# A second Strassen level over pairs of inner blocks in the gate and up products

## The chip, the cores and the metric

One core of a Trainium2 chip runs one program. The metric is the device time of an execution in microseconds (us); several executions are timed, and the median is compared. One further execution was recorded by the hardware profiler: its trace gives the start and the length of each instruction on each engine (TensorE or PE, VectorE or DVE, ScalarE or ACT, GpSimd or POOL, SyncE or SP) and of each DMA.

## The reference, cut to what matters

```python
g = sigmoid((x * gate_w).sum(-1, keepdims=True))       # x: 2048 x 640
a = Cr @ (x @ Wr.T) - Ci @ (x @ Wi.T)                  # C: 2048 x 2048, W: 640 x 640
b = (gelu(x @ w_gate) * (x @ w_up)) @ w_down           # inner width 1728
return g * a + (1 - g) * b
```

All in float32. The change lies in the products with w_gate and w_up.

## The kernel before

The kernel works transposed: the 640 features lie in five blocks of 128 partitions, the 2048 tokens in four tiles of T = 512 columns. Two neighbouring tiles make a token pair (tp 0 and 1). Every float32 operand is split in two parts, a high one (`high`, a copy on ACT to the type fp32r) and the rest (`low`, a subtraction on DVE), and each product is three matmuls (`mm3`, lines 85 to 87): high by high, high by low, low by high, each 128x128 by 128x512 into one PSUM bank.

The inner width 1728 is 13 blocks of 128 and a rest. Block 0 and the rest are done plainly at the start. For each of the blocks f = 1 to 12, `gate_up` (line 271) computes the gate's and the up part's output for one token pair by one level of Strassen's scheme in Winograd's form: the left matrix is the two by two of (gate, up) by (features 0 and 1, features 2 and 3), the right one is (the same features) by (the two token tiles); feature 4 is added plainly (`u5`, `g5`, `D`). Seven products of two feature blocks go to the banks X, Z and V. The sums of the left side come from `load_w` (line 198), the sums T1 to T4 of the right side were made at the start by `load_x`. gate_up is a generator of seven steps, and the loop takes a step of token pair 0 and one of token pair 1 in turn:

A11 to X (copied to s1); S1 and u5 to Z (copied to s5); S2 added to X (copied to s2); A12 and g5 to V (s1 += V, gelu); S3 added to X (s5 += X); S4 and D added to Z (s2 += Z, gelu, times s5); A22 and u5 added to X (s1 *= X).

Two blocks, 2k + 1 and 2k + 2, are one unit for the next product: their outputs and some differences of them go through `keep` (a DMA on POOL's queue) to the DRAM tensors hA and hT, from which the next stage, the product with w_down (`load_k`, `split_k`, `step_k`), loads them. The differences of the second block need s2 and s5 of the first, which are held in `hid`.

Around these products the loop does other stages' work: `sum_wd` and `sum_wu` load weights of later products, form four sums and write them to DRAM; `load_z` loads a block of 128 tokens, multiplies it by the gate row (line 390) and adds it up (line 391); `gate_rows` makes the gate from that. Before the change there is one such sum and up to two gate tiles behind each block.

All larger tiles share one ring of 48 slots of 4 KB a partition (`slot`, `pair`), tiles of 512 columns share 12 (`mtile`), small weight tiles 4 (`wsmall`), and all PSUM tiles the 8 banks (`bank`). An instruction that writes a new tile, or a DMA that fills one, waits until a slot of the ring has no more readers. In the loop the order of each engine's instructions is made by the program's planner from the order of the code and its own durations; SP issues the loads in one order and waits for each one's slot.

Of the kernel before, what the change touches and what calls it, by code (L numbers as in the profile page):

```python
# [29 lines left out]
def kernel(  # L30
# [82 lines left out]
    h0 = [dram.tile([P, 4, T], F32, tag=f"h0{p}", name=f"h0{p}") for p in range(2)]  # L113
    wsu, wneg = ([dram.tile([P, 8, P], F32, tag=f"{n}{p}", name=f"{n}{p}") for p in range(ND)] for n in ("wsu", "wneg"))
    uA, uT = ([[dram.tile([P, 4, T], F32, tag=f"u{n}{j}{p}", name=f"u{n}{j}{p}") for p in range(ND)] for j in range(2)] for n in "AT")
    grd, gmd = (dram.tile([1, S], F32, tag=n, name=n) for n in ("grd", "gmd"))
# [82 lines left out]
    def load_w(f):  # L199
        ra, *a = wchunk(f"wa{f}")  # L200
        rb, d = wsmall(F32, f"wb{f}"), wsmall(F32R, f"wd{f}")
        nc.sync.dma_start(ra, wf[f - 1, :, :8])
        nc.sync.dma_start(rb, wf[f - 1, :, 8:])
        sm, *c = wchunk(f"ws{f}")
        g01, g23, u23 = ra[:, 0:2], ra[:, 2:4], ra[:, 5:7]
        high(a[0], ra)
        tt(sm[:, 0:2], rb, u23, op=ALU.add)
        tt(sm[:, 4:6], g01, rb, op=ALU.subtract)
        tt(sm[:, 2:4], sm[:, 0:2], g01, op=ALU.subtract)
        tt(sm[:, 6:8], g23, sm[:, 2:4], op=ALU.subtract)  # L210
# [12 lines left out]
        return W  # L223

    def keep(to, i, src):
        nc.gpsimd.dma_start(to[:, i], src)  # L226
# [51 lines left out]
    def gate_up(f, W, B, tp, s5):  # L278
# [53 lines left out]
            hid[tp] = s2, s5  # L332
        yield

    def sums_left(n, r, a21, to):

        sm = slot(F32, [P, 8, P], f"{n}s")
        a11, a12, a22 = r[:, 0:2], r[:, 2:4], r[:, 6:8]
        tt(sm[:, 0:2], a21, a22, op=ALU.add)
        tt(sm[:, 4:6], a11, a21, op=ALU.subtract)  # L340
        tt(sm[:, 2:4], sm[:, 0:2], a11, op=ALU.subtract)
        tt(sm[:, 6:8], a12, sm[:, 2:4], op=ALU.subtract)
        nc.gpsimd.dma_start(to, sm)

    def sum_wd(k):

        r, a21 = slot(F32, [P, 8, P], f"dr{k}"), wsmall(F32, f"da{k}")
        nc.sync.dma_start(r, wd[k, :, :8])
        nc.sync.dma_start(a21, wd[k, :, 8:])
        sums_left(f"d{k}", r, a21, wsd[k])  # L350

    def sum_wu(p):


        r, a21 = slot(F32, [P, 8, P], f"ur{p}"), wsmall(F32, f"ua{p}")
        nc.sync.dma_start(r, wu[p, :, :8])
        nc.sync.dma_start(a21, wu[p, :, 8:])
        if p > 1:
            v, r = r, slot(F32, [P, 8, P], f"un{p}")
# [95 lines left out]
    def load_k(i):  # L455


        tp, b, k = kseq[i]
        n = f"{tp}{b}{k}"
        if k == NK and b:  # L460
            return
        r = slot(F32, [P, 8, P], f"kw{n}")
        if k == NK:
            m = slot(F32, [P, 8, P], f"km{n}")
            nc.sync.dma_start(r[:, :5], wd0)
            for q in range(2):
                nc.sync.dma_start(m[q * FR : (q + 1) * FR, :5], wdr)
            r, src = (r, m), h0[tp]
        elif b:
            nc.sync.dma_start(r[:, 0:2], wd[k, :, 6:8])  # L470
            nc.sync.dma_start(r[:, 2:8], wsd[k][:, 0:6])
            src = hT[tp][k]
        else:
            nc.sync.dma_start(r[:, 0:6], wd[k, :, 0:6])
            nc.sync.dma_start(r[:, 6:8], wsd[k][:, 6:8])
            src = hA[tp][k]
        raw = []
        for q in range(2):
            raw.append(pair(F32, f"kr{n}{q}"))
            nc.sync.dma_start(raw[q], src[:, 2 * q : 2 * q + 2])  # L480
        kraw[i] = r, raw

    def split_k(i):
        tp, b, k = kseq[i]
        n = f"{tp}{b}{k}"
        if k == NK and b:
            ktile[i] = ktile[("left", tp)]
            return
        r, raw = kraw.pop(i)
        W = {}  # L490
# [207 lines left out]
        plain_gate_up(W0, B, 1, 2)  # L698
    Bs.append(B)
    zq = list(range(NS))  # L700
    for f in range(1, NF):
        nxt = load_w(f + 1) if f + 1 < NF else None
        s5 = pair(F32, f"s5{f}")
        work = [gate_up(f, W, Bs[tp], tp, s5[:, tp]) for tp in range(2)]
        for step in range(7):
            for w in work:
                next(w)
            if f == NF - 1:
                if step == 1:
                    split_k(0)  # L710
                if step >= 4:
                    load_k(step - 3)
        if f % 2:
            sum_wd(f // 2)
        elif f <= 2 * ND:
            sum_wu(f // 2 - 1)
        if f == NF - 2:
            gate_rows()
            gm = [gate_tile(gmd, tp, f"gm{tp}") for tp in range(2)]
            load_k(0)  # L720
        for _ in range(2):
            if f > 1 and zq:
                load_z(zq.pop(0))
        W = nxt
    order = ctx.enter_context(ExitStack())
    order.enter_context(in_order(ACT, DVE))
    split_k(1)
# [354 lines left out]
```

## Time and profile before

| | us |
|---|---|
| median of 3 runs | 1030.92 |
| lowest and highest run | 1030.63, 1032.3 |
| the profiled execution | 1031.27 |
| its span, from the first instruction to the last | 1029.5 |

The rows below come from the page of the profiled execution and from answers of its trace. A group of instructions is given by line, engine, operation and tiles; its busy time and the mean length of one stand behind the bar, and then the idle time of the engine just before it. Matmuls overlap, so the distance between two starts tells more than the length of one.

### The profile page before, as it was taken

How to read it: one execution, taken by the hardware profiler on the slowest of the kernel's cores; microseconds unless marked ns; L12 is line 12 of the kernel's file. 1: busy time of each engine (PE TensorE's matmuls, PEld its weight loads, DVE VectorE, ACT ScalarE, POOL GpSimd, SP SyncE). 2: the span in 40 equal slices, each digit the busy share in tenths (PEclk: the TensorE clock that was granted, in tenths of full speed). 3: DMA queues.
4: the chain of work that ended last, by engine and by line, in shares of the span. 5: the costliest groups of instructions: out<-in, count | busy, mean ns of one | idle time of the engine just before them, and what ended most of it. 6: DMA issues, size and time to landing. Idle time of an engine off the chain costs nothing.

```text
span 1029.5 us, 12790 instructions
## 1 busy us (share of the span) xinstructions
PE 1023.9 (99%) x4530; PEld 846.2 (82%) x4530; DVE 770.6 (75%) x1030; ACT 449.6 (44%) x570; POOL 132.2 (13%) x237
## 2 busy tenths in 40 slices
PE   9999999999999999999999999999999999999998
PEld 7888888888888888888888888888888888888887
DVE  6998675767654967986798975796678769697775
ACT  5453334343523546556345443343344344365430
POOL 0012121212121200100010011002000200021013
PEclk9999999999999999999999999999999999999999
DMA  8246644746446997878866577557656878897748
GB/s 299 74 153 219 221 169 160 239 160 240 154 148 215 381 346 242 276 253 287 288 216 206 209 224 280 178 198 245 257 177 217 273 275 278 288 328 212 283 94 133
DMA packets 78609, 234.05 MB, mean 227 GB/s; under 512 B 10096, under 2 KB 18320, under 8 KB 78544
## 3 DMA queue, kind: packets, MB, share of 16 engines
q1 hardware_dynamic: 57968, 169.31, 48.6%
q0 software_dynamic: 20432, 63.73, 18.4%
q8 instruction: 35, 0.57, 0.2%
q14 instruction: 30, 0.25, 0.1%
q10 hardware_dynamic: 144, 0.20, 0.1%
HBM read 169.21 MB, written 63.98 MB: 227 GB/s over the span
## 4 chain that ended last, share of the span: by engine, by line
PE 98%; DMA 1%; DVE 0%; ACT 0%; issue 0%; SPq 0%; ACTq 0%
PE pX L85 8%; PE pX L86 8%; PE pX L87 8%; PE pZ L86 5%; PE pZ L85 5%; PE pZ L87 5%; PE pV L86 3%; PE pV L85 3%; PE pV L87 3%; PE pL L85 3%; PE pL L87 3%; PE pL L86 3%; PE pY L87 1%; PE pY L85 1%; PE pR L87 1%; PE pR L85 1%
## 5 line engine op out<-in xcount | busy, mean ns | idle before, releaser
L74 ACT ACTIVATE ch<-csa 128x1024 fp32r<-128x1024 f32 x32 | 34.0, 1063 | 88.4 <-DVE csa L436 53.4
L131 ACT ACTIVATE s<-pX 128x512 f32<-128x512 f32 x64 | 37.8, 596 | 77.2 <-PE pX L87 69.2
L74 ACT ACTIVATE ch<-cra 128x1024 fp32r<-128x1024 f32 x32 | 33.9, 1058 | 47.4 <-PE pL L86 21.6
L77 DVE TENSOR_TENSOR cl<-crb,ch 128x1024 fp32r<-128x1024 f32 x32 | 39.1, 1221 | 17.0 <-ACT ch L74 9.7
L77 DVE TENSOR_TENSOR cl<-cra,ch 128x1024 fp32r<-128x1024 f32 x32 | 39.1, 1222 | 15.5 <-ACT ch L74 15.1
L86 PE MATMUL pL<-cl,xah 128*128 128x512 f32 x128 | 49.8, 389 | 0.0
L87 PE MATMUL pL<-ch,xal 128*128 128x512 f32 x128 | 49.8, 389 | 0.0
L85 PE MATMUL pL<-ch,xah 128*128 128x512 f32 x128 | 49.3, 389 | 0.0
L226 POOL DMA_DIRECT2D hA<-s x48 | 26.1, 544 | 177.0 <-DVE s L313 170.6
L303 DVE TENSOR_TENSOR s<-s,pV 128x512 f32<-128x512 f32 x24 | 16.3, 683 | 41.8 <-PE pV L87 17.6
L77 DVE TENSOR_TENSOR cl<-csb,ch 128x1024 fp32r<-128x1024 f32 x32 | 39.2, 1224 | 6.3 <-ACT ch L74 4.7
L74 ACT ACTIVATE ch<-crb 128x1024 fp32r<-128x1024 f32 x32 | 33.8, 1055 | 21.0 <-DVE cl L77 7.8
L77 DVE TENSOR_TENSOR cl<-csa,ch 128x1024 fp32r<-128x1024 f32 x32 | 39.1, 1221 | 4.0 <-ACT ch L74 3.3
L74 ACT ACTIVATE ch<-csb 128x1024 fp32r<-128x1024 f32 x32 | 33.9, 1059 | 11.9 <-PE pL L86 6.9
L77 DVE TENSOR_TENSOR kl<-kw,kh 128x1024 fp32r<-128x1024 f32 (+1 forms) x26 | 31.4, 1208 | 10.0 <-ACT kh L74 10.0
L74 ACT ACTIVATE kh<-kw 128x1024 fp32r<-128x1024 f32 (+1 forms) x26 | 27.3, 1048 | 11.6 <-DMA kw<-wsd 7.3
L312 ACT ACTIVATE s<-s 128x512 f32<-128x512 f32 x24 | 15.2, 633 | 38.8 <-DVE s L311 38.8
L788 POOL DMA_DIRECT2D uA<-s x16 | 8.7, 542 | 159.3 <-DVE s L834 152.5
L87 PEld LDWEIGHTS pL<-ch,xal 128*128 128x128 f32 x128 | 24.0, 188 | 5.0
L86 PEld LDWEIGHTS pL<-cl,xah 128*128 128x128 f32 x128 | 24.0, 188 | 5.0
L85 PEld LDWEIGHTS pL<-ch,xah 128*128 128x128 f32 x128 | 24.0, 188 | 5.0
L226 POOL DMA_DIRECT2D hT<-s x48 | 26.0, 543 | 14.9 <-DVE s L317 3.9
(3584 smaller groups left out, 3332.6 us busy)
## 6 DMA issues: line engine op xcount, KB each, us to landing
cra<-in_ct SPq DMA_DIRECT2D x64, 512.0 KB, 3.9
crb<-in_ct SPq DMA_DIRECT2D x64, 512.0 KB, 4.8
hA<-s POOLq DMA_DIRECT2D x48, 256.0 KB, 4.7
hT<-s POOLq DMA_DIRECT2D x48, 256.0 KB, 4.8
kr<-hA SPq DMA_DIRECT2D x24, 512.0 KB, 7.8
kr<-hT SPq DMA_DIRECT2D x24, 512.0 KB, 6.5
ux<-uA SPq DMA_DIRECT2D x24, 512.0 KB, 5.5
ux<-uT SPq DMA_DIRECT2D x16, 512.0 KB, 7.1
```

Of the source, the lines that this page charges most:

```text
L74: nc.scalar.activation(hi, raw, AF.Copy)
L77: nc.vector.tensor_tensor(lo, raw, hi.bitcast(F32), op=ALU.subtract)
L85: nc.tensor.matmul(ps, lh, rh, start=first, stop=False, skip_group_check=True)
L86: nc.tensor.matmul(ps, lh, rl, start=False, stop=False, skip_group_check=True)
L87: nc.tensor.matmul(ps, ll, rh, start=False, stop=last, skip_group_check=True)
L131: nc.scalar.activation(m, src, AF.Copy)
L226: nc.gpsimd.dma_start(to[:, i], src)
L303: tt(s1, s1, V, op=ALU.add)
L312: nc.scalar.activation(s2, s2, AF.Gelu_apprx_tanh)
L788: nc.gpsimd.dma_start(to[:, i], src)
```

## The change

Blocks 3 to 12 are taken in five pairs. `gate_up` stays for blocks 1 and 2. In a pair, the first products of both blocks with both token pairs (A11 and A12 of gate_up) are one two by two matrix of features by blocks times one of features by token pairs, and `pair_first` does them by seven products for each of the features' two halves J, where there were eight. A product's running sum is copied on by ACT from one PSUM bank to a new one (`seed`), into which matmuls go on adding. `chain` and `last_products` do what is left of gate_up for one block and one token pair in four steps: S1, S2, S3, and S4 with A22.

The left side's sums over the two blocks are made by `pair_parts`; `chain_parts` and `plain_parts` make what `load_w` made. The right side's sums over the two token pairs are made once by `cross_sums`, during blocks 1 and 2: one stays in place of a part of x that is no longer needed, three for each J are written to DRAM (`xtd`), and each pair loads the six again by `load_cross`, into slots of the ring.

The other stages' sums and gate tiles are moved into the first block of each pair (`extras`, eleven of them), gate_rows and the first load of the next stage into the middle and the end of block 11. A gate tile's product and its addition are one instruction. wsmall has six tiles, and `warm` takes a slot of the ring.

```diff
@@ wsmall, load_z, warm
-        return pool.tile([P, 2, P], dt, tag="w", name=name, bufs=4)
+        return pool.tile([P, 2, P], dt, tag="w", name=name, bufs=6)
...
-        nc.vector.tensor_tensor(r, r, gwb, op=ALU.mult)
-        nc.vector.tensor_reduce(z[:, sb : sb + 1], r, axis=mybir.AxisListType.X, op=ALU.add)
+        nc.vector.tensor_tensor_reduce(r, r, gwb, 1.0, 0.0, ALU.mult, ALU.add, z[:, sb : sb + 1])
...
-    warm = pool.tile([P, T], BF16, tag="warm", name="warm")
+    warm = slot(BF16, [P, T], "warm")
@@ weights of a pair
+    def chain_parts(f, raw, W):
...
+        sm, *c = wchunk(f"ws{f}")
...
+        split(*c, sm)
+        tt(rb[:, 1], ra[:, 4], ra[:, 7], op=ALU.subtract)
+        split(d[:, 0], d[:, 1], rb[:, 1])
...
+    def plain_parts(f, ra):
+        a = slot(F32R, [P, 2, 4, P], f"wp{f}")
+        split(a[:, 0], a[:, 1], ra[:, 4:8])
...
+    def pair_parts(p, r0, r1):
+        a, b = (r[:, 0:4].rearrange("q (j k) c -> q k j c", j=2) for r in (r0, r1))
+        sm = slot(F32, [P, 4, 2, P], f"vs{p}")
+        h, l = slot(F32R, [P, 4, 2, P], f"vh{p}"), slot(F32R, [P, 4, 2, P], f"vl{p}")
+        e, q = slot(F32R, [P, 2, 4, P], f"ve{p}"), pool.tile([P, 2, 2, P], F32R, tag="m", name=f"vq{p}", bufs=12)
...
+        split(h, l, sm)
+        split(e[:, 0], e[:, 1], r0[:, 0:4])
+        split(q[:, 0], q[:, 1], b[:, 1])
@@ sums over the token pairs
+    def cross_sums(J):
+        r = [pair(F32, f"xc{J}{q}") for q in range(2)]
+        for q in range(2):
+            nc.sync.dma_start(r[q], xt[2 * q, 2 * J - 2 : 2 * J].rearrange("d p c -> p d c"))
...
+        for k, (a, b) in enumerate(((h, h2), (l, l2))):
+            nc.gpsimd.dma_start(xtd[J][:, 0:2, k], a.bitcast(F32))
+            nc.gpsimd.dma_start(xtd[J][:, 2, k], b.bitcast(F32))
+        return b12
+    def load_cross(J, i):
+        tcross[J, i] = slot(F32R, [P, 2, T], f"xx{J}{i}")
+        nc.sync.dma_start(tcross[J, i].bitcast(F32), xtd[J][:, {1: 0, 4: 1, 2: 2}[i]])
@@ the products
+    def seed(ps, name):
+        b = bank(name)
+        nc.scalar.activation(b, ps, AF.Copy)
+        return b
+    def pair_first(p, WP, W):
...
+        m(va, 2, "a11", "b11", True)
+        v00 = seed(va, f"pv00{p}")
+        m(xa_, 1, "a11", "b11", True)
+        X[0, 0] = seed(xa_, f"px00{p}")
+        m(ve, 2, "s1", "t1", True)
+        sv = copy(ve, f"sv{p}")
+        m(v00, 2, "a12", "b21")
+        m(xe, 1, "s1", "t1", True)
+        sx = copy(xe, f"sx{p}")
+        m(va, 2, "s2", "t2")
+        v01 = seed(va, f"pv01{p}")
+        m(X[0, 0], 1, "a12", "b21")
+        s1[0, 0] = copy(X[0, 0], f"s100{p}")
+        m(xa_, 1, "s2", "t2")
+        X[0, 1] = seed(xa_, f"px01{p}")
+        fifth(v00, 0, 0)
+        gated(s1[0, 0], v00)
+        m(v01, 2, "s4", "b22")
+        m(va, 2, "s3", "t3")
+        v10 = seed(va, f"pv10{p}")
+        m(X[0, 1], 1, "s4", "b22")
+        tt(X[0, 1], X[0, 1], sx, op=ALU.add)
+        s1[0, 1] = copy(X[0, 1], f"s101{p}")
+        m(xa_, 1, "s3", "t3")
+        X[1, 0] = seed(xa_, f"px10{p}")
+        tt(xa_, xa_, sx, op=ALU.add)
+        X[1, 1] = xa_
+        s1[1, 1] = copy(xa_, f"s111{p}")
+        fifth(v01, 0, 1)
+        gated(s1[0, 1], v01, sv)
+        m(v10, 2, "a22", "t4")
+        fifth(v10, 1, 0)
+        m(X[1, 0], 1, "a22", "t4")
+        s1[1, 0] = copy(X[1, 0], f"s110{p}")
+        gated(s1[1, 0], v10)
+        fifth(va, 1, 1)
+        gated(s1[1, 1], va, sv)
+    def chain(f, W, B, tp, s5, X, s1):
...
+        prod(Z, "S1", "T1", True)
+        mm3(Z, W["u5"], x2, False, True)
+        nc.scalar.activation(s5, Z, AF.Copy)
+        yield
+        prod(X, "S2", "T2", False)
+        s2 = copy(X, f"s2{n}")
+        yield
+        prod(X, "S3", "T3", False)
+        tt(s5, s5, X, op=ALU.add)
+        yield
+        prod(Z, "S4", (2, 2), False)
+        mm3(Z, W["D"], x2, False, True)
+        tt(s2, s2, Z, op=ALU.add)
+        last_products(X, W, B, tp, k, second, s1, s2, s5, prod)
+        yield
@@ the loop over pairs
+    for p in range(1, NK):
+        f = 2 * p + 1
+        for J in (2, 1):
+            load_cross(J, 4)
+        X, s1 = pair_first(p, WP, Ws)
+        for i in range(2):
+            s5 = pair(F32, f"s5{f + i}")
+            work = [chain(f + i, Ws[i], Bs[tp], tp, s5[:, tp], X[i, tp], s1[i, tp]) for tp in range(2)]
+            for step in range(4):
+                for w in work:
+                    next(w)
+                if (i, step) == (0, 0):
+                    chain_parts(f + 1, raws[1], Ws[1])
+                if i == 0 and step in (1, 3):
+                    extras()
...
+                if (i, step) == (0, 2):
+                    nraws = load_raw(f + 2), load_raw(f + 3)
+                if (i, step) == (1, 0):
+                    raws = nraws
+                    WP = pair_parts(p + 1, raws[0][0], raws[1][0])
+                if (i, step) == (1, 1):
+                    nWs = [plain_parts(f + 2 + i, raws[i][0]) for i in range(2)]
+                    for J in (2, 1):
+                        load_cross(J, 1)
+                if (i, step) == (1, 2):
+                    chain_parts(f + 2, raws[0], nWs[0])
+                    load_cross(2, 2)
+                if (i, step) == (1, 3):
+                    load_cross(1, 2)
+                    Ws = nWs
```

## Rows read from the trace of the kernel before

**Rows 1.** The page's parts 1 and 4: busy time of the engines, and the chain.

```profile
PE 1023.9 (99%) x4530; PEld 846.2 (82%) x4530; DVE 770.6 (75%) x1030; ACT 449.6 (44%) x570; POOL 132.2 (13%) x237
...
PE 98%; DMA 1%; DVE 0%; ACT 0%; issue 0%; SPq 0%; ACTq 0%
```

**Rows 2.** All waits of PE: for whom, us in total, times, longest.

```profile
PE pwarm L656 <- DVE warm L613: 1.2, 1, 1.2
PE pm L263 <- ACT x011h L74: 0.5, 1, 0.5
PE kX L85 <- ACT ks L131: 0.3, 1, 0.3
```

**Rows 3.** The table of stretches: block 2, blocks 3 and 4, two of the next stage.

```profile
core 0: us, PE busy (x) PEld busy (x) DVE busy (x) ACT busy (x) POOL busy (x), PEclk, DMA share, GB/s
72.40:96.90 24.50, 24.50 (x110) 20.30 (x109) 20.51 (x38) 9.60 (x15) 4.25 (x9) 1.00 0.61 202
96.20:145.20 49.00, 49.00 (x218) 40.59 (x217) 34.62 (x61) 16.84 (x26) 9.86 (x19) 1.00 0.54 189
...
340.00:360.00 20.00, 20.00 (x90) 16.55 (x89) 18.98 (x20) 12.88 (x14) 4.44 (x9) 1.00 1.04 377
341.10:1029.50 688.40, 684.52 (x3047) 567.51 (x3046) 532.74 (x642) 310.65 (x356) 69.73 (x118) 1.00 0.73 245
```

**Rows 4.** The timeline of PE in block 2 and at its border with block 3.

```profile
85.32 0.39 PE L85 MATMUL pX<-xT03h,ws2h 128*128 128x512 f32 x1
...
88.04 0.39 PE L85 MATMUL pZ<-x022h,ws2h 128*128 128x512 f32 x1
...
95.97 0.39 PE L87 MATMUL pX<-x15h,wa2l 128*128 128x512 f32 x1
96.20 0.39 PE L85 MATMUL pX<-x011h,wa3h 128*128 128x512 f32 x1
```

**Rows 5.** The timeline of PE and of ACT: the end of a product and its copy.

```profile
100.73 0.39 PE L87 MATMUL pZ<-x05h,wa3l 128*128 128x512 f32 x1
...
101.16 0.60 ACT L296 ACTIVATE s<-pZ 128x512 f32<-128x512 f32 x1 [1.44 <-PE pZ L87]
```

**Rows 6.** Groups of DVE by line and shape in blocks 3 and 4.

```profile
L324 DVE TENSOR_TENSOR s<-s,pX 128x512 f32<-128x512 f32 x5 | 3.4, 682 | 0.1
L390 DVE TENSOR_TENSOR xz<-xz,gwb 128x640 f32<-128x640 f32 x4 | 3.3, 816 | 0.0
L391 DVE TENSOR_REDUCE z<-xz 128x1 f32<-128x640 f32 x4 | 3.2, 810 | 0.0
...
L77 DVE TENSOR_TENSOR wa5l<-wa5r,wa5h 128x1024 fp32r<-128x1024 f32 x1 | 1.2, 1218 | 0.0
...
L209 DVE TENSOR_TENSOR ws5r<-ws5r,wa5r 128x256 f32<-128x256 f32 x1 | 0.4, 418 | 0.0
```

**Rows 7.** Groups of ACT by line and shape in blocks 3 and 4.

```profile
L131 ACT ACTIVATE s<-pX 128x512 f32<-128x512 f32 x8 | 4.8, 598 | 10.1 <-PE pX L87 7.3 <-DMA hA<-s 2.8
L312 ACT ACTIVATE s<-s 128x512 f32<-128x512 f32 x4 | 2.5, 634 | 5.5 <-DVE s L311 5.5
...
L74 ACT ACTIVATE ws5h<-ws5r 128x1024 fp32r<-128x1024 f32 x1 | 1.1, 1064 | 0.0
...
L74 ACT ACTIVATE wd<-wb 128x128 fp32r<-128x128 f32 x2 | 0.6, 312 | 5.3 <-DVE wb L213 5.3
```

**Rows 8.** Line 202, the loads of a block's weights (512 KB each): issue to landing.

```profile
DMA to landing us min/median/max: 3.7/5.2/7.3
```

**Rows 9.** The timeline of SP, and SP's waits in the loop for line 202.

```profile
104.46 0.33 SPq L202 DMA_DIRECT2D wa5r<-in_wf  x1
...
SPq L202 <- DMA hT<-s: 15.3, 4, 7.4
```

**Rows 10.** The timeline of PE at the start of the program.

```profile
5.42 0.63 PE L263 MATMUL pg<-x011h,w0h 128*128 128x512 f32 x1
5.84 0.63 PE L263 MATMUL pu<-x011h,w0h 128*128 128x512 f32 x1
```

More of the change, by code (lines that the diff above doesn't have):

```diff
@@ L115 @@
     uA, uT = ([[dram.tile([P, 4, T], F32, tag=f"u{n}{j}{p}", name=f"u{n}{j}{p}") for p in range(ND)] for j in range(2)] for n in "AT")
+    xtd = {J: dram.tile([P, 3, 2, T], F32, tag=f"xtd{J}", name=f"xtd{J}") for J in (1, 2)}
     grd, gmd = (dram.tile([1, S], F32, tag=n, name=n) for n in ("grd", "gmd"))
@@ L223, in load_w, with load_raw @@
         return W
+    def load_raw(f):
+        ra, rb = slot(F32, [P, 8, P], f"wa{f}"), wsmall(F32, f"wb{f}")
+        nc.sync.dma_start(ra, wf[f - 1, :, :8])
+        nc.sync.dma_start(rb, wf[f - 1, :, 8:])
+        return ra, rb
+    def chain_parts(f, raw, W):
+        ra, rb = raw
+        sm, *c = wchunk(f"ws{f}")
+        g01, g23, u23 = ra[:, 0:2], ra[:, 2:4], ra[:, 5:7]
+        tt(sm[:, 0:2], rb, u23, op=ALU.add)
+        tt(sm[:, 4:6], g01, rb, op=ALU.subtract)
+        tt(sm[:, 2:4], sm[:, 0:2], g01, op=ALU.subtract)
+        tt(sm[:, 6:8], g23, sm[:, 2:4], op=ALU.subtract)
+        d = wsmall(F32R, f"wd{f}")
+        split(*c, sm)
+        tt(rb[:, 1], ra[:, 4], ra[:, 7], op=ALU.subtract)
+        split(d[:, 0], d[:, 1], rb[:, 1])
+        W["D"] = d[:, 0], d[:, 1]
+        for i in range(2):
+            for k in range(4):
+                W[f"S{k + 1}", i] = at(c, 2 * k + i)
@@ new lines, in cross_sums @@
+    def cross_sums(J):
+        r = [pair(F32, f"xc{J}{q}") for q in range(2)]
+        for q in range(2):
+            nc.sync.dma_start(r[q], xt[2 * q, 2 * J - 2 : 2 * J].rearrange("d p c -> p d c"))
+        b11, b21, b12, b22 = r[0][:, 0], r[0][:, 1], r[1][:, 0], r[1][:, 1]
+        tt(b11, b12, b11, op=ALU.subtract)
+        tt(b12, b22, b12, op=ALU.subtract)
+        tt(b22, b22, b11, op=ALU.subtract)
+        tt(b21, b21, b22, op=ALU.subtract)
+        h, l = hl(f"xU{J}")
+        split(h, l, r[0])
+        h2, l2 = mtile(F32R, f"xh{J}"), mtile(F32R, f"xl{J}")
+        split(h2, l2, b22)
+        for k, (a, b) in enumerate(((h, h2), (l, l2))):
+            nc.gpsimd.dma_start(xtd[J][:, 0:2, k], a.bitcast(F32))
+            nc.gpsimd.dma_start(xtd[J][:, 2, k], b.bitcast(F32))
+        return b12
@@ L225, in keep @@
+    tcross = {}
+    def load_cross(J, i):
+        tcross[J, i] = slot(F32R, [P, 2, T], f"xx{J}{i}")
+        nc.sync.dma_start(tcross[J, i].bitcast(F32), xtd[J][:, {1: 0, 4: 1, 2: 2}[i]])
     def keep(to, i, src):
@@ L333, in gate_up, with m, fifth, gated @@
         yield
+    def seed(ps, name):
[3 more added lines that the diff above has]
+    def pair_first(p, WP, W):
+        b = {J: {"b11": at(Bs[0][J, 1], 0), "b21": at(Bs[0][J, 1], 1), "b22": at(Bs[1][J, 1], 1), "t3": at(Bs[1][J, 1], 0)} for J in (1, 2)}
+        for J in (1, 2):
+            for i in (1, 2, 4):
+                c = tcross.pop((J, i))
+                b[J][f"t{i}"] = c[:, 0], c[:, 1]
+        def m(ps, J, w, x, first=False):
+            mm3(ps, WP[J][w], b[J][x], first, True)
+        def fifth(ps, f, q):
+            mm3(ps, W[f]["g5"], at(Bs[q][5], 0), False, True)
+        def gated(s1, *more):
+            for v in more:
+                tt(s1, s1, v, op=ALU.add)
+            nc.scalar.activation(s1, s1, AF.Gelu_apprx_tanh)
+        va, xa_, ve, xe = (bank(f"p{n}{p}") for n in ("va", "xa", "ve", "xe"))
+        X, s1 = {}, {}
+        m(va, 2, "a11", "b11", True)
[35 more added lines that the diff above has]
+        gated(s1[1, 1], va, sv)
+        return X, s1
@@ new lines, in chain, with prod @@
+    def chain(f, W, B, tp, s5, X, s1):
+        n = f"{f}_{tp}"
+        Z = bank(f"pZ{n}")
+        x1, x2 = at(B[5], 0), at(B[5], 1)
+        k, second = divmod(f - 1, 2)
+        def prod(ps, a, b, first):
+            for i in range(2):
+                mm3(ps, W[a, i], at(B[b], i), first and i == 0, True)
+        prod(Z, "S1", "T1", True)
[13 more added lines that the diff above has]
+        yield
@@ new lines, in last_products @@
+    def last_products(X, W, B, tp, k, second, s1, s2, s5, prod):
+        nc.scalar.activation(s2, s2, AF.Gelu_apprx_tanh)
+        tt(s2, s2, s5, op=ALU.mult)
+        keep(hA[tp][k], 1 + 2 * second, s2)
+        if second:
+            h12, t1 = hid.pop(tp)
+            tt(h12, s2, h12, op=ALU.subtract)
+            keep(hT[tp][k], 2, h12)
+            tt(t1, s2, t1, op=ALU.subtract)
+            keep(hT[tp][k], 1, t1)
+        prod(X, "A22", "T4", False)
+        mm3(X, W["u5"], at(B[5], 0), False, True)
+        tt(s1, s1, X, op=ALU.mult)
+        keep(hA[tp][k], 2 * second, s1)
+        if second:
+            tt(s5, s1, t1, op=ALU.subtract)
+            keep(hT[tp][k], 3, s5)
+        else:
+            tt(s5, s2, s1, op=ALU.subtract)
+            keep(hT[tp][k], 0, s5)
+            hid[tp] = s2, s5
@@ L700, with extras @@
     zq = list(range(NS))
-    for f in range(1, NF):
-        nxt = load_w(f + 1) if f + 1 < NF else None
+    sq = [lambda k=k: sum_wd(k) for k in range(NK)]
+    for p in range(ND):
+        sq.insert(2 * p + 1, lambda p=p: sum_wu(p))
+    def extras():
+        sq.pop(0)()
+        for _ in range(2):
+            if zq:
+                load_z(zq.pop(0))
+    t3 = {}
+    W2 = load_w(2)
+    for f in (1, 2):
         s5 = pair(F32, f"s5{f}")
@@ L707 @@
                 next(w)
[L708 to L723, printed above, removed]
@@ L724 @@
-        W = nxt
+            if (f, step) in ((1, 3), (2, 0)):
+                J = 3 - f
+                t3[J] = cross_sums(J)
+            if f == 2 and step == 2:
+                raws = load_raw(3), load_raw(4)
+        W = W2
+    WP = pair_parts(1, raws[0][0], raws[1][0])
+    for J in (1, 2):
+        split(Bs[1][J, 1][0][:, 0], Bs[1][J, 1][1][:, 0], t3[J])
+    Ws = [plain_parts(3 + i, raws[i][0]) for i in range(2)]
+    for i in (1, 2):
+        for J in (2, 1):
+            load_cross(J, i)
@@ new lines @@
+    chain_parts(3, raws[0], Ws[0])
+    for p in range(1, NK):
[3 more added lines that the diff above has]
+        X, s1 = pair_first(p, WP, Ws)
+        for i in range(2):
+            s5 = pair(F32, f"s5{f + i}")
[7 more added lines that the diff above has]
+                    extras()
+                if p == NK - 1:
+                    if (i, step) == (0, 2):
+                        extras()
+                        gate_rows()
+                        gm = [gate_tile(gmd, tp, f"gm{tp}") for tp in range(2)]
+                    if (i, step) == (0, 3):
+                        load_k(0)
+                    if (i, step) == (1, 0):
+                        split_k(0)
+                    if i == 1 and step >= 1:
+                        load_k(step)
+                    continue
+                if (i, step) == (0, 2):
+                    nraws = load_raw(f + 2), load_raw(f + 3)
+                if (i, step) == (1, 0):
+                    raws = nraws
+                    WP = pair_parts(p + 1, raws[0][0], raws[1][0])
+                if (i, step) == (1, 1):
+                    nWs = [plain_parts(f + 2 + i, raws[i][0]) for i in range(2)]
+                    for J in (2, 1):
+                        load_cross(J, 1)
[5 more added lines that the diff above has]
+                    Ws = nWs
```

13 lines of the change are left out of this document (added).

## The prediction

> **What bounds the kernel now.** Read the busy times first: TensorE (PE) is busy 99% of the span, VectorE (DVE) 75%, ScalarE (ACT) 44%, and the chain that ended last is 98% PE [rows 1]. A busy PE need not be a PE at its pace, so read the waits next: over the whole span PE waited for others 2.0 us in three places, none of them in the gate/up loop [rows 2]. Then the timeline: matmuls start 0.2267 us apart (12 in 2.72 us), and the last of one block is followed by the first of the next at the same distance [rows 4]. So in this loop each matmul costs 0.2267 us and nothing else costs anything; a change can gain by taking matmuls out, and everything else in it can only lose. Last, the table of stretches: a pair of inner blocks (49.0 us) has DVE at 34.6 us, ACT at 16.8 to 18.3 and the DMA engines at 0.54 of their time with 189 GB/s; the stage behind it also runs PE without a gap [rows 3], so what is gained here stays gained to the end.
>
> **Part 1, matmuls.** Before, one block and one token pair take 18 products of 3 matmuls, 54; two blocks and two token pairs 216. After, pair_first has 14 products `m` and 4 `fifth`, 54 matmuls, and each of four chains 13 products, 39: 54 + 156 = 210. Five pairs (blocks 3 to 12; blocks 1 and 2 keep the old form) save 30 matmuls, 30 x 0.2267 = **6.8 us**. This has one answer.
>
> **Part 2, ACT and DVE work, hidden by their idle time.** Per pair ACT goes from 20 operations of 128x512 to 28 (6 seeds, 6 copies, 4 + 4 gelus, 4 + 4 copies of the chains): 8 x 0.6 = +4.8 us; its splits of weights go from four wide and two narrow ones to three wide, three of 512, one of 256 and two narrow ones, about +1.1 us. That makes ACT some 24 of 47.6 us. DVE goes from 28 additions and products to 32 (+4 x 0.68 = 2.7 us); the weights' sums and low halves from 9.4 to 12.3 us (+2.9); four gate reductions lose one of their two operations, 4 x 0.81 = -3.2 us if the merged one takes what the product takes, 0 if it takes both [rows 6, 7]. So 37 to 40 of 47.6 us. Both stay under PE's time: cost 0. A seed is ACT writing PSUM, which no row shows; the nearest is the PSUM-to-SBUF copy of 0.598 us [rows 7], and I bound it at 0.4 to 1.06 us (the row of the wide split) and take 0.6. In the stretch of block 2 DVE had 20.5 of 24.5 us busy [rows 3]; there the two cross_sums (4.2 us each), the pair's first sums and splits take the place of load_w(3), load_w(4), two sums and two gate tiles, about 17 us for about 17 us: cost 0, and if that cover fails it delays the first pair once, by 1 to 3 us.
>
> **Part 3, new short distances between PE and ACT.** ACT starts 0.43 us after the start of the last matmul of a product (100.73 to 101.16) [rows 5] and takes 0.6, so a copy is done 1.03 us after that start. In pair_first the fourth product needs the first seed; between lie two products, so it starts 7 x 0.2267 = 1.59 us after the same point: 0.56 us of room. The later seeds have 1.2 us or more. In chain, S3 now follows S2 directly (A12 stood between): the copy of X after S2 of one token pair must be done before S3 of that pair, again with 0.56 us of room. That is 5 tight points in a pair, 25 in all. If ACT has just begun a wide split (1.06 us), the point loses 0.5 us: bounds 0 and 12.5 us. Queued behind such a wait is all of PE. ACT has some three wide operations in 47.6 us, so a collision is rare: I take 0.02 us a point, 0.5 us. Nothing suggests a gain here: no wait of PE is left to remove.
>
> **Part 4, the cross tiles, the real risk.** A pair reads six tiles of 512 KB back from DRAM: 3.1 MB on top of 189 GB/s x 49 us = 9.3 MB, so about 260 GB/s, below the 377 that a stretch behind shows with PE full [rows 3]. Bandwidth is no bound; the moment of issue is. A load is issued when one of the 48 slots is free. Count them in step 2 of the second block: 32 hold the split x parts and sums, 1 the gate row; the current pair still holds 2 + 1 weight tiles and two s5; the next pair holds two raw tiles, 3 of pair_parts, 2 of plain_parts and the two first cross tiles: 47. Still wanted before the border are chain_parts' three and two cross tiles. So some wait for the next release: S4's weights of the second block, free 12 matmuls = 2.7 us before the border. Tile (2,2) is first read after 5 products (3.4 us), tile (1,2) after 7 (4.8), (2,4) after 14 (9.5), (1,4) after 16 (10.9). The last two can have the slots that the first two tiles leave at 2.0 and 3.4 us. Room from release to use: 6.1, 7.5, 7.5 and 7.5 us. Loads of 512 KB in this loop landed in 3.7 to 7.3 us, median 5.2 [rows 8], and issuing takes 0.33 [rows 9]. So the median fits everywhere, and the longest is late by 1.5 us at the first. I take 0.25 us a border, 1.0 us for four; the bounds are 0 and the case of rival 1. The Trainium skill, "DMA: Bandwidth & Descriptors", section on the anatomy of one DMA, gives about 2.0 us plus bytes over 436 GB/s; for 512 KB that is an estimate of 3.2 us, every tile would be there, and the sum would be the whole 6.8 us less 0.5. The rows disagree (5.2), and I go by them.
>
> **Part 5, moves.** The down and hidden-DFT sums (loads on SP, writes on POOL) and the gate tiles come as eleven `extras`, two a pair and one more, instead of one a block: the same instructions, past the same queues, in the half of a pair in which no cross tile is needed soon. gate_rows and the first load_k come in the middle of block 11 instead of behind it, so the next stage's loads start earlier: 0. Cross_sums' eight writes are on POOL, which is busy 9.9 of 49 us [rows 3], 20 us and more before they are read. The six small tiles and `warm` in a slot: 0.
>
> **Sum.** 1029.5 us of span - 6.8 + 0.5 + 1.0 = 1024.2. The profiled execution lasted 1031.27, 1.77 more than its span: 1026.0. The median of the runs, 1030.92, lies 0.35 below that execution, so the forecast is **1025.6**.
>
> **Rival 1, slower: cross tiles wait for a slot that a write must empty.** The place is the border of pairs. The other slots in question there are the two s5 tiles, which are written to DRAM at the end of a pair. The trace shows what a load that takes such a slot gets: wa5r was issued at 104.46, though the pair had ended at 96.20 [rows 4, 9], 8.3 us later, and four loads of this line waited for these writes, 15.3 us together [rows 9]. If tile (2,4) gets this slot it lands at 8.3 + 0.3 + 5.2 = 13.8 us, needed at 9.5: 4.3 us, at four borders 17 us, so 1025.6 - 1.0 + 17 = 1042. It decides from 1.4 us lost a pair (6.8 / 5). For it: 52 tiles want 48 slots, and SP issues in order. Against it: six slots come free between -2.7 and +4.2 us (S4's two, the second block's plain tile, three cross tiles) before s5's do, and in the trace such waits never reached PE [rows 2]. Chance 0.17.
>
> **Rival 2, no change: the tight points of part 3 take the gain.** If half the bound is met at each of 25 points (0.25 us), 6.25 us go: about 1030.9 with the rest as summed. For it: ACT has half its time full. Against: what runs there is short, and an operation of 0.6 us in the way costs 0.1 at most. Chance 0.08.
>
> **Rival 3, no change: it does what it says, and the next stage waits out the gain.** PE reaches the down product 6.8 us earlier, in a stretch where the DMA engines are full (1.04, 377 GB/s) and DVE has 19.0 of 20 us busy [rows 3]. If those and not PE set the pace there, the gain is given back: 1030.9. Against: load_k moves forward by more than that, and PE has no wait there now [rows 2]. Chance 0.08.
>
> **Rival 4, slower: the clock.** The trace shows the lower pace once, in the first 7 us, after PE had stood still for data: starts 0.42 us apart, as at 1.2 GHz (the stretch's granted clock doesn't show it), where 0.2267 belongs to 2.4 [rows 10, 4]. Eleven or so matmuls ran so, 0.2 us lost each. If each of five borders brought one such fall, 5 x 2.2 = 11 us: 1036. That needs PE to stand still at the borders, so it comes only behind rival 1 or 2. Chance 0.03. The Trainium skill, "TensorE: Matmul & The Clock Gate", section on psum-queue depth-cycling, has a rule of this kind: cycling through banks makes PE idle briefly between groups, and the clock swings. Before, PE cycles through 12 banks a pair and the granted clock is 1.00 in all stretches [rows 3], so the trace doesn't bear it out.
>
> **How the numbers follow.** The forecast with its losses of 0 to 4 us has 0.64. About 0.2% (2 us) is what a measurement of this kernel can tell from no change. Faster 0.64, same 0.16 (rivals 2 and 3), slower 0.20 (rivals 1 and 4). Low end: the whole 6.8 us from the fastest run, 1023.4 with a little over; high end 1033.0, where rival 1 has lost 2.5 us a border more than forecast; beyond it stay about 0.15 above and 0.04 below.
>
> **What would show it.** Right: 4500 matmuls, PE still at 99%, starts still 0.2267 us apart through pair_first, a pair in 47.6 us instead of 49.0, and PE's waits in the loop under 2 us. Part 3 wrong: waits of PE on ACT at the S3 products or the fourth product of a pair. Part 4 wrong, rival 1: waits of PE for tiles xx, or products of a chain drawn ahead, with SP's loads of xx waiting for the hT writes. Rival 3: the same loop shorter, and waits at the kX, kL products. Rival 4: starts 0.43 us apart behind a border. The count of part 1 is certain; the prediction would be wrong by what PE waits.

## The result and the profile after

The changed kernel took 1034.29 us (median of 9; 1032.22 to 1037.43), the kernel before 1030.92: a ratio of 1.0036, with a 95% interval of 1.0023 to 1.0049. So it is slower by some 3.4 us where 1025.6 was forecast. With six later executions the median of 15 is 1034.83.

The page of the profiled execution (1032.22 us, span 1030.5), part 1, and then all waits of PE (for whom, us in total, times, longest):

```profile
PE 1020.1 (99%) x4500; PEld 840.2 (82%) x4500; DVE 795.2 (77%) x1099; ACT 478.4 (46%) x631; POOL 136.9 (13%) x245
```

```profile
PE pva L87 <- DVE ve L77: 2.8, 1, 2.8
PE pxa L85 <- DVE s L499: 1.3, 1, 1.3
PE pwarm L850 <- DVE warm L807: 1.2, 1, 1.2
PE pv L85 <- ACT pv L414: 0.6, 2, 0.3
PE pm L340 <- ACT x011h L74: 0.5, 1, 0.5
```

The matmuls are 4500, as the sum had it [rows 1], but the loop, which had no wait of PE [rows 2], now has four. A wait in this list is only the idle part. What a place costs is read from the starts of matmuls, as their distance less 0.2267 us each: from the first matmul of block 1 to the first of the next stage 9.0 us are lost, against 0.4 before. That is the 6.8 us and more. Three places carry it.

**The first border, 4.9 us.** The timeline of PE (start, length, engine, line, operation, tiles, the idle time before it and its releaser), then that of DVE:

```profile
95.20 0.39 PE L85 MATMUL pva<-x021h,ve 128*128 128x512 f32 x1
95.42 0.39 PE L86 MATMUL pva<-x021l,ve 128*128 128x512 f32 x1
98.62 0.50 PE L87 MATMUL pva<-x021h,ve 128*128 128x512 f32 x1 [2.81 <-DVE ve L77]
...
100.39 0.63 PE L85 MATMUL pve<-xx,vh 128*128 128x512 f32 x1
100.82 0.63 PE L86 MATMUL pve<-xx,vh 128*128 128x512 f32 x1
101.24 0.63 PE L87 MATMUL pve<-xx,vl 128*128 128x512 f32 x1
```

```profile
90.73 1.23 DVE L77 TENSOR_TENSOR vl<-vs,vh 128x1024 fp32r<-128x1024 f32 x1 [0.53 <-ACT vh L74]
91.87 0.69 DVE L390 TENSOR_TENSOR s<-s,s 128x512 f32<-128x512 f32 x1
...
97.28 0.68 DVE L401 TENSOR_TENSOR s<-s,pX 128x512 f32<-128x512 f32 x1
97.88 0.69 DVE L77 TENSOR_TENSOR ve<-wa,ve 128x512 fp32r<-128x512 f32 x1
```

The third matmul of the first pair needs the low half of `ve`. DVE works without a pause from 90.73 on, and ten operations of block 2's tail stand ahead of that half. PE waits 3 us, and behind the wait matmuls start 0.43 us apart, where 0.2267 belongs.

**The seeds, 1.7 us in four pairs.** PE and ACT at the border of the first and second pair:

```profile
148.17 0.39 PE L87 MATMUL pva<-x021h,ve 128*128 128x512 f32 x1
148.38 0.63 ACT L509 ACTIVATE s<-s 128x512 f32<-128x512 f32 x1 [3.69 <-DVE s L503]
...
148.85 0.39 PE L87 MATMUL pxa<-x011h,ve 128*128 128x512 f32 x1
148.92 0.58 ACT L414 ACTIVATE pv<-pva 128x512 f32<-128x512 f32 x1
...
149.55 0.50 PE L85 MATMUL pv<-x021h,ve 128*128 128x512 f32 x1 [0.32 <-ACT pv L414]
149.89 0.40 PE L85 MATMUL pve<-xx,vh 128*128 128x512 f32 x1
```

The first matmul of the fourth product (`pv`) stands ahead of the third product (`pve`), which isn't the order of the code: the planner drew it forward. So the seed has 4 matmuls' time and not 7, and a gelu of the pair before stands ahead of it on ACT. Starts of 148.85 and 149.55 and then 0.34 to the next: 0.59 us lost, in the other pairs 0.59, 0.26 and 0.27.

**The last block, 1.6 us here.** SP's wait in this stretch, then DVE, then PE:

```profile
SPq L578 <- DMA gmd<-gr: 21.5, 1, 21.5
```

```profile
333.62 1.22 DVE L77 TENSOR_TENSOR kl<-kw,kh 128x1024 fp32r<-128x1024 f32 x1 [1.82 <-ACT kh L74]
336.06 1.23 DVE L77 TENSOR_TENSOR kb0000l<-kr,kb0000h 128x1024 fp32r<-128x1024 f32 x1 [1.22 <-ACT kb0000h L74]
337.93 1.22 DVE L77 TENSOR_TENSOR kb0001l<-kr,kb0001h 128x1024 fp32r<-128x1024 f32 x1 [0.64 <-ACT kb0001h L74]
339.07 0.68 DVE L499 TENSOR_TENSOR s<-s,pxa 128x512 f32<-128x512 f32 x1
```

```profile
338.10 0.39 PE L87 MATMUL pZ<-x15h,wd 128*128 128x512 f32 x1
339.80 0.50 PE L85 MATMUL pxa<-xT14h,wp 128*128 128x512 f32 x1 [1.32 <-DVE s L499]
```

SP stands 21.5 us for the gate row's way through DRAM; the next stage's loads are queued behind it and are issued from 321.01 on. DVE waits for what they bring, three times, and the sum s5 += X (line 499), for which PE waits, stands behind those splits.

The kernel before had SP's wait as well, and a longer one, and its loads went out later than here, without a loss. What differs is when the tiles are there. The wait, and then the first load and ACT's first split of what the loads bring, before:

```profile
SPq L383 <- DMA gmd<-gr: 34.6, 1, 34.6
```

```profile
322.90 0.37 SPq L474 DMA_DIRECT2D kw<-in_wd  x1
329.03 1.06 ACT L74 ACTIVATE kh<-kw 128x1024 fp32r<-128x1024 f32 x1 [1.06 <-DMA kw<-wsd]
```

The same two in the changed kernel, 11.5 us apart and not 6.1:

```profile
321.01 0.52 SPq L668 DMA_DIRECT2D kw<-in_wd  x1
332.52 1.06 ACT L74 ACTIVATE kh<-kw 128x1024 fp32r<-128x1024 f32 x1 [1.27 <-DMA kw<-wsd]
```

### The profile page after: what moved, and what is told of

It is laid out like the page before. It is cut to its first block, busy times and chain, and to the rows that moved or that the text cites. A ratio compares the mean times of both kernels' runs of the same rounds, so it can differ in the third digit from the quotient of the medians.

```text
span 1030.5 us, 12985 instructions
## 1 busy us (share of the span) xinstructions
PE 1020.1 (99%) x4500; PEld 840.2 (82%) x4500; DVE 795.2 (77%) x1099; ACT 478.4 (46%) x631; POOL 136.9 (13%) x245
## 4 chain that ended last, share of the span: by engine, by line
PE 93%; DVE 3%; DMA 2%; ACT 1%; issue 1%; SPq 0%; ACTq 0%; DVEq 0%
PE pZ L85 4%; PE pZ L87 4%; PE pZ L86 4%; PE pX L85 4%; PE pX L86 3%; PE pX L87 3%; PE pL L86 3%; PE pL L85 3%; PE pL L87 3%; PE px L85 2%; PE px L87 2%; PE px L86 2%; PE pV L86 2%; PE pV L85 2%; PE pV L87 2%; PE pY L86 1%
## 5 line engine op out<-in xcount | busy, mean ns | idle before, releaser
L74 ACT ACTIVATE ch<-crb 128x1024 fp32r<-128x1024 f32 x32 | 33.8, 1056 | 20.9 <-DVE cl L77 7.8
L509 ACT ACTIVATE s<-s 128x512 f32<-128x512 f32 x20 | 12.6, 630 | 50.3 <-DVE s L503 50.3
L629 DVE TENSOR_TENSOR csa<-cra 128x512 f32<-128x512 f32 x32 | 22.0, 686 | 8.2 <-PE pL L86 6.5
L743 POOL DMA_DIRECT2D out<-ks x12 | 6.5, 540 | 163.7 <-DVE ks L742 163.0
```

What stands on the lines that cost most here:

```text
L74: nc.scalar.activation(hi, raw, AF.Copy)
L509: nc.scalar.activation(s2, s2, AF.Gelu_apprx_tanh)
L629: tt(s1[:, 0], r1[:, 1], r1[:, 0], op=ALU.subtract)
L743: nc.gpsimd.dma_start(out[2 * tp + t, e], src)
```

## The experiments

The theory: these three places are the loss, each with its own cause (DVE's order, PE's order, SP's queue). Rivals: the cross tiles (rival 1 of the prediction), and the clock (rival 4).

**The changed kernel again.** No edit, timed, and later once more for a profile.

> The changed kernel once more, unaltered, for the spread of its time: nine executions lay between 1032.2 and 1037.4 us, and the one that was profiled was the shortest. If the three places that this profile shows (about 4.7 us at the border of blocks 2 and 3, 1.9 us at the seeds of the four later pairs, 1.6 us in the last block) make the whole loss, then a longer execution has longer waits at these same places. If cross tiles that land late do it (rival 1 of the prediction), a longer execution shows TensorE waiting for tiles xx at the later borders. If it is the clock (rival 4), it shows matmuls 0.43 us apart in more places than the one at 100 us. Expected: 1034 us, and in the profile waits at the three places.

> The changed kernel once more, for a profile of another execution. 14 executions so far lay between 1032.2 and 1037.4 us; two profiles, of 1032.2 and 1034.7 us, show 1.3 and 2.1 us of waiting in the last block, and 4.9 and 4.5 us lost at the first border. If the last block's wait makes the spread, a longer execution shows it longer, and above some 2.8 us with a fall of the clock behind it. If the first border makes it, more matmuls at 0.43 us stand there than 11.

Measured: 1035.53 (1034.38 to 1035.83) and 1034.83. Both profiles show the same three places; the last block differs most: 2.3 us lost in the first. In the second a wait of 2.2 us and, for the first time there, the slow pace behind it:

```profile
338.57 0.39 PE L87 MATMUL pZ<-x15h,wd 128*128 128x512 f32 x1
341.17 0.50 PE L85 MATMUL pxa<-xT14h,wp 128*128 128x512 f32 x1 [2.21 <-DVE s L499]
341.50 0.59 PE L86 MATMUL pxa<-xT14l,wp 128*128 128x512 f32 x1
341.89 0.63 PE L87 MATMUL pxa<-xT14h,wp 128*128 128x512 f32 x1
342.31 0.63 PE L85 MATMUL pxa<-xT14h,wp 128*128 128x512 f32 x1
```

That place lost 4.0 us, so 1.6 to 4.0 in three executions; no other place in the loop differs as much between them. In the first one PE also waited 0.7 us for a cross tile, once, at the first border; and in both the program's start was 1.0 us longer than in the profile above (see the end).

**The first seed's room.**

```diff
-        m(v00, 2, "a12", "b21")
         m(xe, 1, "s1", "t1", True)
         sx = copy(xe, f"sx{p}")
+        m(v00, 2, "a12", "b21")
```

> The fourth product of pair_first, the one that accumulates on the first seed, trades places with the product behind it, so the seed has 1.24 us of room where it had 0.56. If the short room at the seed costs what the profile shows at the four later pairs (0.58, 0.58, 0.26, 0.26 us and 0.23 once), the time falls by about 1.7 to 1.9 us to 1032.5, and the waits of TensorE for ScalarE at this product are gone. If the loss is elsewhere (first border, cross tiles, clock), the time stays within 0.5 us of 1034.3.

Measured: 1034.74 us, and 0.59, 0.59, 0.27 and 0.27 us lost at the same matmul. A miss: in the built kernel only the product's second and third matmul had moved, the first still stood ahead of the third product. The edit to test was PE's order itself:

```diff
-        X, s1 = pair_first(p, WP, Ws)
+        with in_order(PE):
+            X, s1 = pair_first(p, WP, Ws)
```

> The changed kernel with the third edit alone: TensorE kept in pair_first's written order. If the drawn-ahead first matmul of the fourth product is the whole cause at the seeds, the waits of 0.26 to 0.59 us there vanish in the profile at all five pairs, and the time is 1.9 us under the changed kernel's (1034.3 to 1035.5), so about 1033. If ScalarE is the cause, 0.3 us remain at the second and third pair. The first border (4.5 to 4.9 us) and the last block (1.6 to 2.5 us) stay as they are; if the time falls by more, the three places are not separate.

Measured: 1032.67 us (12 executions), 2.2 under the changed kernel's 1034.83. The waits at the seeds are gone in all pairs, though the gelu still stands ahead of the second pair's seed (at 148.31); what is left are 0.16 to 0.25 us once in each of pairs 2 to 4, at a product of a cross tile. The second pair's seed on ACT, and the fourth product's first matmul:

```profile
148.85 0.58 ACT L414 ACTIVATE pv<-pva 128x512 f32<-128x512 f32 x1
149.69 0.39 PE L85 MATMUL pv<-x021h,ve 128*128 128x512 f32 x1
```

The room of 0.56 us that the prediction counted was enough, once it was there.

**The first border.** In block 2's loop, with the call behind the loop taken out:

```diff
+            if f == 2 and step == 3:
+                WP = pair_parts(1, raws[0][0], raws[1][0])
```

> The sums and splits of the first pair's weights are issued within block 2 (behind its fourth step) and not behind its last, so that they stand in VectorE's order ahead of the block's last products. If the cover that failed at the first border is VectorE's order, the 3.0 us wait of TensorE for the low half of ve and the matmuls at 0.43 us behind it are both gone: about 4 to 4.7 us less, 1030 us. If the lower clock there came without the wait, only some 3 us go, 1031.3. If the first border is not what makes the loss, within 0.5 us of 1034.3; if VectorE is merely short of time there, the wait moves to the next product and the gain is 0 to 1.5 us.

Measured: 1029.89 us, 4.9 less. On DVE the half that PE waited for now follows directly:

```profile
91.19 1.23 DVE L77 TENSOR_TENSOR vl<-vs,vh 128x1024 fp32r<-128x1024 f32 x1 [0.53 <-ACT vh L74]
92.33 0.68 DVE L77 TENSOR_TENSOR ve<-wa,ve 128x512 fp32r<-128x512 f32 x1
```

The wait and the slow matmuls are both gone. DVE does the same work as in the changed kernel (20.9 of 25 us busy around block 2 in both), so it was the order and not a lack of time. But 1.2 us are lost some 10 us later at the cross tiles, for which the wait had left more time.

**The last block.** The gate tiles' loads moved behind `load_k(3)`:

> The two loads of the gate tiles in the last pair are issued behind the four loads of the next stage's operands and not ahead of them, so that the DMA queue's engine doesn't stand for the gate rows' way through DRAM while the other loads are queued behind it. If that wait (21.5 us) is what made the loads bunch and VectorE come late in the last block, the 1.58 us of TensorE there go: about 1032.7, and the spread of the runs shrinks, since landing times under a full queue vary. If the spread comes from elsewhere, the median falls by 1.6 us but the runs still spread over 5 us. If the loss is at the first border or at the cross tiles only, within 0.5 us of 1034.3.

Measured: 1031.34 us (1030.06 to 1033.69), 3.5 less. The next stage's first load goes out at 308.35 instead of 321.01, and the last block has no wait:

```profile
308.35 0.39 SPq L668 DMA_DIRECT2D kw<-in_wd  x1
```

The other way round, `split_k(0)` moved behind `load_k(3)` and the loads left where they were:

> The changed kernel with the splits of the next stage's first operands issued at the end of the last pair, and the gate tiles' loads where they were, ahead of the others. VectorE's order in the last block is then the one that the later gate loads gave too. If the loss in the last block (1.3 to 2.2 us of waiting, growing in longer executions) comes from those splits standing ahead of the block's own sums, it is gone here as well and the time is that of the later gate loads, 1031.3. If it comes from the loads being issued late, the wait moves to VectorE's next operation that needs one (the sums of the down weights) or to the first down products, and the time stays at 1033.5 to 1035.

Measured: 1039.42 us, 4.6 more, beyond both of the cases expected. The waits of PE between 335 and 352 us:

```profile
PE kX L86 <- DVE kb0000l L77: 2.2, 1, 2.2
PE kX L85 <- ACT kb0000h L74: 1.8, 1, 1.8
PE kZ L85 <- ACT kb0001h L74: 0.2, 1, 0.2
```

The block's own sums are in time now, and the next stage waits instead, with 11 slow matmuls behind it: 7.4 us. So the cause is that what the loads bring comes late; the place in DVE's order only chooses who waits.

**Two and three edits together.**

> The two edits together: the first pair's weight sums within block 2, and the gate tiles' loads behind the next stage's loads. Alone they gave 1029.9 and 1031.3 us against 1034.3 to 1035.5 of the changed kernel. If the two places are separate losses, the sum is about 4.5 + 3.3 us: 1026.7 us, faster than before by 0.4%. If the second border's wait only moves (what PE gains early it waits out at the last block), about 1029.5. If cross tiles late at the first border (0.9 to 1.2 us in two profiles) grow once the first wait is gone, 1028 with a wide spread.

> The two edits and, third, TensorE kept in pair_first's written order. In the changed kernel the first matmul of the fourth product stands ahead of the third product on TensorE, so that the first seed has no room where the prediction counted 0.56 us. If the losses of 0.26 to 0.59 us a pair at this place come from that order, about 1.9 us less than with two edits: 1024.8 us. If they come from ScalarE standing in a long operation, the written order gives back only the 0.26 of each, some 1.2 us: 1025.5. If holding the order takes away fillers that now hide other waits (cross tiles at products 14 and 16 of pair_first), no gain or a loss of 1 us against the two edits: 1026.7 to 1027.7.

Measured: 1027.53 and 1027.42 us, 0.9967 (0.9955 to 0.9979) and 0.9969 (0.9957 to 0.9981) of the kernel before: both beat both kernels. The medians do not show the third edit, for which 1024.8 was expected. The trace does, if it is read from the first matmul of block 3 to the first of the next stage, which leaves out the program's start (see the end) and the later stages:

| profiled execution | us, from block 3 to the next stage | of it lost |
|---|---|---|
| before | 245.0 | 0.1 |
| changed, three profiles | 246.8, 248.0, 248.6 | 8.7, 10.0, 10.6 |
| first border | 243.2 | 5.1 |
| gate loads late | 245.1 | 7.0 |
| PE's order | 245.8 | 7.8 |
| two edits | 241.6 | 3.6 |
| three edits | 239.9 | 1.9 |
| three, and cross sums early | 239.3 | 1.3 |
| three, and no cross loads | 238.4 | 0.4 |

The last column is the first less 1050 x 0.2267 = 238.0 us (before: 1080 matmuls, 244.8). The third edit is worth 1.7 us here.

**Without the cross tiles' loads.** The three edits, and pair_first multiplies resident tiles instead of the cross tiles, so the sums over the two token pairs are left out of these products:

> The three edits, and the cross tiles are not read back from DRAM: pair_first multiplies resident tiles in their place (its results are left wrong in these products), so 30 loads of 512 KB and their six slots a pair are gone. If the cross tiles cost what rival 1 of the prediction says at every border, this is several us faster than the three edits; if they cost only at the first border, 0.3 to 1 us faster and with less spread; if their 15.7 MB of traffic slowed other loads (the last block's included), more than the waits for xx show. Expected: 0.5 us below the three edits, 1024.3.

Measured: 1025.30 us, 2.1 under the three edits (1.5 in the table); the five executions of the two overlap. A pair takes 47.6 us. All waits of PE that are left:

```profile
PE pwarm L848 <- DVE warm L805: 1.2, 1, 1.2
PE pm L339 <- ACT x011h L74: 0.4, 1, 0.4
PE kX L85 <- ACT ks L132: 0.4, 1, 0.4
```

So the cross tiles cost 1.5 to 2.1 us once nothing else is late, 0.9 of it at the first border, and not the 17 of rival 1. Last, the cross sums at steps 1 and 4 of block 1 instead of step 3 of block 1 and step 0 of block 2:

> The three edits, and the cross tiles' sums made and written to DRAM some 10 us earlier (in the second and fifth step of block 1). With three edits the loads of the first pair's cross tiles waited 14.4 us for that write, and TensorE waited 0.6 us for the last tile. If the write's end sets when those tiles come, they come earlier, TensorE's wait for xx at the first border is gone, and the time is 0.6 to 0.9 us less: 1026.6. If the slots set it (the last two tiles take the slots of the first two, which are read only at the border), the wait stays: 1027.4. If VectorE, full in that stretch, now comes late in block 1, slower: 1028.5.

Measured: 1027.09 us, 0.9967 of before (0.9955 to 0.9980). PE's list of waits has no cross tile at the first border any more, though 0.5 us are still lost there; a new wait of 0.8 us for ACT's split `wa2h` stands at the begin of block 2, which the table leaves out. The gain of 0.3 us is within the spread.

**Stalls of chosen length.** The three edits, ACT kept in pair_first's order too, and the first seed repeated:

```diff
         v00 = seed(va, f"pv00{p}")
+        for _ in range({2: 4, 3: 5, 4: 6, 5: 8}.get(p, 0)):
+            nc.scalar.activation(v00, va, AF.Copy)
```

> The three edits, with the first seed of pairs 2 to 5 copied 4, 5, 6 and 8 times more, so that TensorE stands still before the fourth product: at about 0.53 us a copy, less the room of 0.56, for 1.6, 2.1, 2.6 and 3.7 us. If the lower clock behind the first border was brought on by standing still for 2.8 us, then matmuls 0.43 us apart follow the longest stall, and none follow the two short ones, as none followed the 1.3 to 2.2 us in the last block; some 10 of them would add 2 us. If that border's clock fell for another reason (what ran before it, the transfers there), all matmuls behind the four stalls are 0.2267 us apart. Time: about 10 us of stalls over the three edits, 1037.5, and 2 to 4 us more with the clock.

Measured: 1044.67 us, in one execution; the stalls came out 0.2 to 0.6 us longer than planned. The timeline of PE at the four stalls, and the table of stretches around the third (columns as in [rows 3]; the third value from the end is the granted clock):

```profile
149.71 0.50 PE L85 MATMUL pv<-x021h,ve 128*128 128x512 f32 x1 [1.81 <-ACT pv L443]
150.05 0.40 PE L86 MATMUL pv<-x021l,ve 128*128 128x512 f32 x1
...
200.30 0.50 PE L85 MATMUL pv<-x021h,ve 128*128 128x512 f32 x1 [2.70 <-ACT pv L443]
200.64 0.40 PE L86 MATMUL pv<-x021l,ve 128*128 128x512 f32 x1
...
251.19 0.80 PE L85 MATMUL pv<-x021h,ve 128*128 128x512 f32 x1 [2.99 <-ACT pv L443]
251.78 0.63 PE L86 MATMUL pv<-x021l,ve 128*128 128x512 f32 x1
...
306.11 0.80 PE L85 MATMUL pv<-x021h,ve 128*128 128x512 f32 x1 [4.22 <-ACT pv L443]
306.71 0.63 PE L86 MATMUL pv<-x021l,ve 128*128 128x512 f32 x1
```

```profile
250.00:252.00 2.00, 0.81 (x2) 0.72 (x3) 0.13 (x1) 1.97 (x4) 0.39 (x2) 0.60 1.01 406
252.00:254.00 2.00, 2.00 (x6) 1.52 (x6) 0.00 (x0) 0.13 (x1) 0.51 (x1) 0.50 1.02 418
```

Behind 1.8 and 2.7 us the pace is full at once; behind 3.0 and 4.2 us 13 and 12 distances of 0.43 us follow, at a granted clock of 0.50, which is 1.2 of 2.4 GHz: 2.8 and 2.7 us more than behind the two short ones. So standing still is enough to bring the clock down, at a place where it fell in no other kernel.

## Why the prediction was wrong, point by point

**Part 1 was right.** 4500 matmuls, and with nothing late a pair takes the 47.6 us that it named. In the kernel without cross loads the five pairs lost only 0.4 us over that, and its time, 1025.3, lies near the forecast; that is partly luck, since it leaves out the cross loads, for which the forecast had 1.0 us.

**Part 2 failed, and this is the largest step.** It compared sums: 20.5 of 24.5 us busy before [rows 3], 17 us of new work for 17 of old, so "cost 0". But the old work had no date in that stretch, and the new one has: the first pair's parts are read by PE at the border's first matmul. DVE was able to do it all and did it in the wrong order. The text named this case ("if that cover fails it delays the first pair once, by 1 to 3 us"), gave it no term in the sum and left out what follows it: 4.9 us lost, of which 3.0 is the wait and 1.9 the clock and the restart. The sizes were right: a seed took 0.58 us (0.6 taken), DVE was busy 36.8 to 38.0 of 48 us in each of the four stretches of that length from 105 us on (37 to 40 forecast), and ACT 21.4 to 23.0 in three of them and 26.3 in the fourth (24); the merged gate operation took 0.82 and a second one of 0.08, which saves 0.73 of the 0.81 assumed.

**Part 3 was mis-sized at one of its two kinds of points.** The 20 points at S3 cost nothing. The 5 seeds, taken at 0.02 us each, cost 0.26 to 0.59 at four of them, 1.7 us in all. The room of 0.56 us was counted from the order of the code, while PE's order is the planner's.

**Part 4 had the size about right and the place wrong.** 1.0 us for four borders was taken; taking the loads out gives back 1.5 to 2.1. Most of it stands at the first border, which the part didn't count, where the last two tiles go into the slots of the first two, as it described. The thirty loads, six a pair, landed in 3.6 to 8.5 us, median 5.8, where it took 5.2 and a longest of 7.3 [rows 8]. The estimate of 3.2 us by the Trainium skill, "DMA: Bandwidth & Descriptors", section on the anatomy of one DMA, lies below all thirty of them. The page fits it to a DMA that GpSimd issues, and by size alone; these loads are issued by SP, and the DMA engines were busy 0.67 to 0.75 of the four stretches named in part 2.

**Part 5 failed.** "So the next stage's loads start earlier: 0" looked at the place in the code and not at when the tiles land. SP is one queue, and in both kernels it stands for gate_rows' row to go to DRAM and back through the gate tiles' loads, so the loads went out only 1.9 us earlier than before (321.01 and 322.90). The moved sums then went out in the same stretch, 324 GB/s between 319 and 329 us where it had been 232, and the next stage's tiles landed in 12.0 us (median) where it had been 8.7. Sending the loads out 12.7 us sooner took the loss away. That the traffic of the moved sums made the tiles late fits these rows, but no run left it out. Cost 1.6 to 4.0 us in three executions, and a part of the spread: with the late gate loads eleven executions lie within 3.6 us, where fifteen of the changed kernel lie within 5.2.

**The rivals.** Rival 1 (1042) has no row for it: no load of a cross tile waited for an hT write in any run. Some waited for a slot that another sum's write had to empty (1.1 and 1.7 us), and behind the first border no list of PE's waits has a cross tile. Rival 2 named the right kind of place and found 1.7 of its 6.25 us. Rival 3 is out: from the first down product to the end the two kernels need 688.4 and 688.5 us, so a gain in the loop stays. Rival 4 had the mechanism, "starts 0.43 us apart behind a border", and its condition, PE standing still, and tied it to rivals 1 and 2; it came with part 2's failure, once or twice an execution and not five times. The cause in its sentence on the Trainium skill, "TensorE: Matmul & The Clock Gate", section on psum-queue depth-cycling, is not seen: the pairs behind the first run through the banks at a granted clock of 1.00, and in the loop it fell only behind a stall.

Two sums of the prediction are off in themselves: with 6.25 us lost rival 2 comes to 1025.6 - 0.5 + 6.25 = 1031.4 and not 1030.9, and 2.5 us more at each of four borders give 1035.6, while the high end of 1033.0 is 1.9 us a border.

The sum, made again with what was measured: 1026.0 (the forecast for the profiled execution) - 1.5 for the terms of parts 3 and 4, + 4.9 + 1.7 + 0.2 (one late cross tile) + 1.6 = 1032.9, where the profiled execution took 1032.2 with a start that was 1.0 us shorter than in the one of before.

## What to carry to other kernels

Work that is hidden by a busy share is hidden only if it stands in time in its engine's queue: for each moved or added operation look for its first reader and for what is planned ahead of it on the same engine. Count room between engines in the order that was built, not in that of the code. A load that waits for a round trip through DRAM belongs behind the loads that are due sooner.

## What the runs showed of the hardware

A stall of PE costs more than its length: the first distance after it is 0.34 and not 0.2267 us, and behind 3.0 and 4.2 us of standing still some 12 matmuls run at half pace (2.8 and 2.7 us more). 1.8 and 2.7 us brought no fall; the 2.8 us at the first border brought 5 to 8 slow distances in each of the seven profiles that have it, and 2.2 us in the last block brought 8 in one and none in another, so length alone doesn't decide.

The program's first 10 us hold between none and 11 of these slow distances, by execution and not by kernel (three in the one of before; none, three and four in those of the changed kernel): the first matmul of `gate_up` came between 45.7 and 48.3 us. Two kernels' times of single executions can differ by 2.5 us by that alone; the granted clock of those first stretches reads 1.00.
